# The bias of the score sigmoid, as a constant of the instruction instead of a tile

## The chip, the cores and the metric

The kernel runs on one core of a Trainium2 chip. The metric is the device time of one execution in microseconds; lower is better. The kernel before takes 389.12 us (median of three runs, 388.84 to 390.28).

## The reference

Two layers stand one behind the other. The first is attention with a sigmoid in the place of the softmax, on 8 batches of 12 heads, 448 positions and 64 channels:

```
scores = scale * np.matmul(q, k.transpose(0, 1, 3, 2)) - np.log(S)
attn = 1.0 / (1.0 + np.exp(-scores))
attn_out = np.matmul(attn, v)
```

The subtracted logarithm of S = 448 is the same number, about 6.1048, for every score. The second layer is dense, on 3584 tokens of 768 channels (all heads of a position side by side):

```
h = x @ w_in
g = h * (1.0 / (1.0 + np.exp(-beta * h)))
out = g @ w_out
```

`w_in` is 768 x 2048, `w_out` is 2048 x 768, and `beta` has one number per column of `h`. Inputs and output are float32.

## The kernel before

**Loading.** The DMAs that GpSimd issues load q and k (the tile `raw`, lines 105 to 117), v, `w_in` and `w_out`, and turn them into fp16 on the way. Each group of four heads (a "quad", 24 in all, three to a batch) is then transposed by VectorE in blocks of 32 (`qT`, `kT`, lines 179 to 194). SyncE issues only the load of beta and the stores.

**Scores and sigmoid.** `score` (L201) multiplies 32 rows of `kT` with 32 rows of `qT`, for four heads at once in four strips of the array, into a PSUM tile `sco` of two banks (two heads, up to 448 positions each). `weigh` (L212) is one ScalarE activation on that tile: sigmoid(0.125 x score + bias), written as fp16 to `attnT`. It reads the bias from the tile `nlogs`, one float32 per partition, all equal. There are 171 of these activations: 165 on 896 elements per partition and 6 on 448. `visit` and `half_visit` issue the scores of two `sco` tiles and then their two activations, which so come in pairs. In the first stage there are three `sco` tiles, later two, so that the scores of the next visit can begin only when the pair before has read its tiles.

**The weighted sum and the dense layer.** `attend` (L267) multiplies `attnT` with v, and VectorE copies the result to `xT` (L276). `dense1` (L285) is `x @ w_in` into a PSUM bank; ScalarE makes `sg`, the sigmoid with the scale taken from the tile `beta_sb` and a constant bias of zero (L293); VectorE multiplies the two into `gt` (L296), which sets the bank free. `dense2` (L315) is `g @ w_out` for the first three and the last of the 28 row blocks; the others go through seven products of sums in place of eight (`strassen`, L397 with the sums of L386, L416, L419 and L421).

**The order.** It is written out by hand: within `tc.manual_schedule()` each engine executes its instructions in the order in which they are issued in the source. The first stage (lines 496 to 560) loads the quads of batch 0 in halves and fills TensorE's waits with multiplications of a tile of zeros (`idle_units`, L509). After it, the visits of the other quads alternate with units of the dense layer, which a list with costs in microseconds (`filler_stream`, `spread`, `rest`) deals out between them; from line 595 on a visit is followed by so many units as its budget allows. The list and its costs are fixed in the source and do not depend on what an instruction takes on the chip.

**Around the change.** GpSimd's first instructions are two loads, the two `memset` of lines 498 (`nlogs`) and 499 (`dummy`), and then the loads of the second and third quad. The activation on `dummy` (L500) lets ScalarE load its table of functions while the first data are on their way. `nlogs` is the first tile of the pool `const`.

Of the kernel before, what the change touches and what calls it, by code (L numbers as in the profile page):

```python
# [8 lines left out]
FP32 = mybir.dt.float32  # L9
# [4 lines left out]
def kernel(  # L14
# [10 lines left out]
    nc = tc.nc  # L25
# [6 lines left out]
    P = 128  # L32
# [16 lines left out]
    NEG_LOG_S = -math.log(float(S))  # L49
# [3 lines left out]
    const = ctx.enter_context(tc.tile_pool(name="const", bufs=1))  # L53
# [35 lines left out]
        return psum["one"].tile([P, cols], FP32, tag=f"one{i}", name=name)  # L89


    nlogs = const.tile([P, 1], FP32, name="nlogs")
    dummy = const.tile([P, 1], FP32, name="dummy")
    beta_in = const.tile([BLK, P], FP32, name="beta_in")
    beta_sb = const.tile([P, BLK], FP32, name="beta_sb")
# [11 lines left out]
    def load_one(g: int, r: int, c0: int = 0, c1: int = NB):  # L107
        b, t = divmod(g, QPB)
        if g not in raws:
            raws[g] = rawp.tile([P, 2, NB, D], FP16, tag="raw", name="raw")  # L110
        nc.gpsimd.dma_start(  # L111
            out=raws[g][:, r, c0:c1].rearrange("p c d -> p (c d)"),
            in_=(q, k)[r][b, HQ * t : HQ * (t + 1)].rearrange("h (p c) d -> (h p) (c d)", c=NB)[
                :, c0 * D : c1 * D
            ],
        )
# [93 lines left out]
    def weigh(sco, n: int):  # L210
        at = attnp.tile([P, 2, S], FP16, tag="attnT", name="attnT")
        nc.scalar.activation(  # L212
            out=at[:, :, 0:n],
            in_=sco[:, :, 0:n],
            func=AF.Sigmoid,
            bias=nlogs[:, 0:1],
            scale=MSCALE,
        )
        return at


    def visit(g: int, jt: int, also=()):
        if jt < JF:
            todo = [(score_tile(), [s]) for s in (2 * g, 2 * g + 1)]
        else:
            todo = [(score_tile(), [2 * h, 2 * h + 1]) for h in (g, *also)]
        for e in range(PAIR):
            for sco, slots in todo:
                for s in slots:
                    for hh in range(2):  # L230
                        score(sco, 0, s, jt, hh, e, 0, S)
        for sco, slots in todo:
            at = weigh(sco, S)
            for s in slots:
                at_tiles[s, jt, 0] = at


    def half_visit(g: int, c0: int, second: int):
        slots = (2 * g, 2 * g + 1)
        scos = [score_tile() for _ in slots]  # L240
        plan = [(s, jt, sco, jt * QH) for jt in (0, 1) for s, sco in zip(slots, scos)]
        widths = [S, S]
        if second:
            plan = [(s, 2, sco, 0) for s, sco in zip(slots, scos)]
            plan += [(s, JF, scos[0], QH) for s in slots]
            widths = [S, QH]
        for i in range(0, len(plan), 2):
            for e in range(PAIR):
                for s, jt, sco, u0 in plan[i : i + 2]:
                    for hh in range(2):  # L250
                        score(sco, u0, s, jt, hh, e, c0, QH)
        ats = {id(sco): weigh(sco, n) for sco, n in zip(scos, widths)}
        for s, jt, sco, u0 in plan:
            at_tiles[s, jt, c0] = ats[id(sco)][:, :, u0 : u0 + QH]
# [240 lines left out]
    with tc.manual_schedule():  # L495
        load_one(0, 0, 0, NH)
        load_one(0, 1)
        nc.gpsimd.memset(nlogs, NEG_LOG_S)  # L498
        nc.gpsimd.memset(dummy, 0.0)  # L499
        nc.scalar.activation(out=dummy, in_=dummy, func=AF.Sigmoid, bias=0.0, scale=1.0)  # L500

# [156 lines left out]
```

## Time and profile before

| | |
|---|---|
| time, median of three runs | 389.12 us |
| the three runs | 390.28, 389.12, 388.84 us |
| span of the profiled execution | 388.2 us |
| the profiled execution's own time | not listed apart from the three runs; the span is 0.9 us below their median |
| TensorE busy | 381.5 us (98%) |
| ScalarE busy | 241.5 us (62%), of which L212 is 160.3 us |
| VectorE busy | 229.7 us (59%) |
| granted TensorE clock | 1.00 over the span |

The span runs from the first to the last instruction on the core. Around it lies what the trace does not hold, the launch and the end of the program. Busy shares are means over stages with different limits, and TensorE's busy time counts a matmul from its start to a modelled end, in which the next has already begun. What another engine's speed is worth is thus read from the places where TensorE stands still, and from what ended each of them.

### The profile page before, as it was taken

To read this page: it belongs to the slowest core of one execution; us is meant where nothing else is said; L and a number is where in the kernel's file an instruction comes from. 1 tells how busy PE (TensorE), PEld (TensorE's weight loads), DVE (VectorE), ACT (ScalarE), POOL (GpSimd) and SP (SyncE) were. 2 spreads that over 40 slices of the span, in tenths; PEclk is the share of its full clock that TensorE was granted. 3 is DMA by queue.
4 is the path that set the end of the run, shared out by engine and by line. 5 is a ranking of instruction groups with operands and counts; after the bars stand their busy time and mean duration, and the time that the engine had idled before them with its cause. 6 is when DMAs were issued, how large, how long until landed. Compare 5 with 4: busy or idle time off the path is not lost.

```text
span 388.2 us, 7376 instructions
## 1 busy us (share of the span) xinstructions
PE 381.5 (98%) x2991; PEld 191.4 (49%) x2991; DVE 229.7 (59%) x437; ACT 241.5 (62%) x329; POOL 67.3 (17%) x117
## 2 busy tenths in 40 slices
PE   8899999999999999999999999999999999999996
PEld 3477754444545444444554445544445444555563
DVE  2356463885766556655765656664676565655762
ACT  4887865687565796497365783568853677625200
POOL 7833343122110410140110410104100000000000
PEclk9999999999999999999999999999999999999999
DMA  7999999629243760446353561629113300030033
GB/s 112 172 191 203 198 204 199 144 55 112 47 91 70 126 80 14 105 79 66 49 115 74 87 71 34 127 60 144 28 21 83 82 2 2 0 83 0 2 81 122
DMA packets 42401, 34.30 MB, mean 88 GB/s; under 512 B 21872, under 2 KB 38784, under 8 KB 42368
## 3 DMA queue, kind: packets, MB, share of 16 engines
q0 software_dynamic: 36976, 22.81, 42.8%
q1 hardware_dynamic: 5392, 11.02, 11.0%
q8 instruction: 23, 0.38, 0.4%
q14 instruction: 10, 0.08, 0.1%
HBM read 45.62 MB, written 11.01 MB: 146 GB/s over the span
## 4 chain that ended last, share of the span: by engine, by line
PE 93%; DMA 3%; ACT 2%; POOL 0%; issue 0%; DVE 0%; POOLq 0%
PE m_ps L285 39%; PE m_ps L397 29%; PE sco L201 11%; PE av_ps L267 10%; PE m_ps L315 4%; ACT attnT L212 2%; DMA raw<-in_k_dram 2%; DMA v<-in_v_dram 1%; POOL raw L111 0%; PE idle_ps L509 0%; ACT sg L293 0%; DVE osb L328 0%; DVE gt L296 0%; POOL nlogs L498 0%; POOL dummy L499 0%
## 5 line engine op out<-in xcount | busy, mean ns | idle before, releaser
L212 ACT ACTIVATE attnT<-sco,nlogs 128x896 f16<-128x896 f32 (+1 forms) x171 | 160.3, 991 | 84.3 <-PE sco L201 83.5
L285 PE MATMUL m_ps<-xT,w_in 128*128 128x448 f16 (+1 forms) x864 | 154.7, 332 | 0.4 <-DVE gt L296 0.3
L296 DVE TENSOR_TENSOR gt<-m_ps,sg 128x448 f16<-128x448 f32 (+1 forms) x144 | 79.8, 572 | 84.4 <-ACT sg L293 84.3
L285 PEld LDWEIGHTS <-w_in 128*128 128x128 f16 x864 | 80.6, 98 | 70.9 <-issue 15.5
L293 ACT ACTIVATE sg<-m_ps,beta_sb 128x448 f32<-128x448 f32 (+1 forms) x144 | 81.8, 595 | 31.3 <-PE m_ps L285 30.1
L397 PEld LDWEIGHTS <-sum 128*128 128x128 f16 x480 | 45.2, 98 | 36.4 <-issue 7.9
L201 PE MATMUL sco<-qT,kT 32*128 32x448 f16 (+3 forms) x864 | 52.6, 340 | 1.3 <-ACT attnT L212 1.1
L397 PE MATMUL m_ps<-w_T,sum 128*128 128x384 f16 x288 | 51.6, 327 | 0.0
L111 POOL DMA_DIRECT2D raw<-in_q_dram x27 | 14.8, 550 | 189.7 <-DVE kT L191 183.1
L416 DVE TENSOR_TENSOR osb<-m_ps,osb 128x384 f32<-128x384 f32 x60 | 33.3, 555 | 18.7 <-PE m_ps L397 16.9
L267 PE MATMUL av_ps<-attnT,v 128*64 128x448 f16 (+3 forms) x432 | 42.2, 340 | 0.7 <-DMA v<-in_v_dram 0.5
L276 DVE CAST xT<-av_ps 128x448 f16<-128x448 f32 (+1 forms) x54 | 28.8, 568 | 22.5 <-PE av_ps L267 22.5
L386 DVE TENSOR_TENSOR sum<-gt 128x1024 f16<-128x1024 f16 x60 | 39.1, 678 | 0.1
L397 PE MATMUL m_ps<-w_T,gt 128*128 128x384 f16 x192 | 34.2, 327 | 0.0
L397 PE MATMUL m_ps<-w_out,sum 128*128 128x384 f16 x192 | 33.7, 326 | 0.0
L267 PEld LDWEIGHTS <-v 128*64 128x64 f16 (+1 forms) x432 | 19.1, 107 | 25.5 <-issue 16.9
L201 PEld LDWEIGHTS <-kT 32*128 32x128 f16 (+1 forms) x864 | 13.5, 96 | 29.6 <-issue 27.5
L397 PEld LDWEIGHTS <-gt 128*128 128x128 f16 x192 | 18.1, 98 | 14.8 <-issue 3.1
L315 PE MATMUL m_ps<-w_out,gt 128*128 128x384 f16 (+2 forms) x128 | 22.5, 327 | 0.0
L132 POOL DMA_DIRECT2D v<-in_v_dram x32 | 19.8, 635 | 8.0 <-DMA w_in<-in_moe_w_in_dram 5.3
L179 DVE STREAM_TRANSPOSE qT<-raw 128x448 f32<-128x448 f32 (+1 forms) x27 | 16.6, 616 | 4.8 <-DMA raw<-in_q_dram 4.8
L315 PEld LDWEIGHTS <-gt 128*128 128x128 f16 x128 | 11.9, 98 | 10.3 <-issue 3.1
(24 smaller groups left out, 96.9 us busy)
## 6 DMA issues: line engine op xcount, KB each, us to landing
out_dram<-osb SPq DMA_DIRECT2D x98, 96.0 KB, 1.9
raw<-in_k_dram POOLq DMA_DIRECT2D x24, 224.0 KB, 4.8
raw<-in_q_dram POOLq DMA_DIRECT2D x21, 224.0 KB, 3.6
v<-in_v_dram POOLq DMA_DIRECT2D x32, 144.0 KB, 6.6
w_in<-in_moe_w_in_dram POOLq DMA_DIRECT2D x8, 384.0 KB, 10.9
w_out<-in_moe_w_out_dram POOLq DMA_DIRECT2D x4, 768.0 KB, 13.4
v<-in_v_dram POOLq DMA_DIRECT2D x16, 48.0 KB, 6.2
out_dram<-osb SPq DMA_DIRECT2D x2, 384.0 KB, 2.3
```

What stands on the lines that cost most here:

```text
L132: nc.gpsimd.dma_start(out=vs[b][i * BLK : (i + 1) * BLK, :, 0:JF].rearrange("p h j d -> p h (j d)"), in_=rows[:, :, JF * i * D : JF * (i + ...
L201: nc.tensor.matmul(sco[base : base + nk, hh, u0 : u0 + n], kT[g][lo : lo + BLK, jt * P : jt * P + nk, e], qT[g][lo : lo + BLK, c0 : c0 + n ...
L212: nc.scalar.activation(out=at[:, :, 0:n], in_=sco[:, :, 0:n], func=AF.Sigmoid, bias=nlogs[:, 0:1], scale=MSCALE,)
L267: nc.tensor.matmul(av[hh * D : (hh + 1) * D, 0:n], vs[b][base : base + nk, 2 * (s % NPAIR) + hh, jt], at[base : base + nk, hh, 0:n], start ...
L276: nc.vector.tensor_copy(out=xTs[b][:, s % NPAIR, c0 : c0 + n], in_=av[:, 0:n])
L285: nc.tensor.matmul(m1[:, 0:n], w_in16[:, hc, dc * P : (dc + 1) * P], xTs[b][:, hc, c0 : c0 + n], start=(hc == 0), stop=(hc == NHC - 1),)
L293: nc.scalar.activation(out=sg[:, 0:n], in_=m1[:, 0:n], func=AF.Sigmoid, bias=0.0, scale=beta_sb[:, dc : dc + 1])
L296: nc.vector.tensor_tensor(out=gt[:, dc, off : off + n], in0=m1[:, 0:n], in1=sg[:, 0:n], op=ALU.mult)
L315: nc.tensor.matmul(m2, gt[:, dc, cols(t)], w_out16[:, dc, lo:hi], start=(dc == 0), stop=(dc == NDC - 1),)
L386: nc.vector.tensor_tensor(out=sums[t, i], in0=x, in1=y, op=op)
L397: nc.tensor.matmul(m2, (x if op is None else sums[t, i])[:, dc], w[:, dc], start=first and dc == 0, stop=(dc == ND - 1), skip_group_check= ...
L416: nc.vector.tensor_tensor(out=out, in0=in0, in1=in1, op=op)
```

## The change

The activation of `weigh` takes its bias from the instruction, as a float constant, in place of the tile. The tile `nlogs` and its `memset` go.

```
-    nlogs = const.tile([P, 1], FP32, name="nlogs")
     dummy = const.tile([P, 1], FP32, name="dummy")
...
             func=AF.Sigmoid,
-            bias=nlogs[:, 0:1],
+            bias=NEG_LOG_S,
             scale=MSCALE,
...
         load_one(0, 1)
-        nc.gpsimd.memset(nlogs, NEG_LOG_S)
         nc.gpsimd.memset(dummy, 0.0)
```

In the built program, 171 activations have a constant operand where they had an access pattern, GpSimd has one instruction less, and the activation on `dummy` waits for GpSimd's count to be 1 where it was 2. Every other instruction, its engine, its place and its waits stay as they were. The tiles move in one respect: the pool places tiles in steps of 32 bytes per partition, so each tile behind `nlogs` (all but the constants ahead of it) starts 32 bytes lower in its partition: `w_in16` at 17184 in place of 17216, `gt` at 66336 in place of 66368. In the kernel before the starts of the large tiles are multiples of 64; in the kernel after each is 32 off such a multiple.

More of the change, by code (lines that the diff above doesn't have):

```diff
@@ L89, in bank @@
         return psum["one"].tile([P, cols], FP32, tag=f"one{i}", name=name)
-    nlogs = const.tile([P, 1], FP32, name="nlogs")
     dummy = const.tile([P, 1], FP32, name="dummy")
@@ L215, in weigh @@
             func=AF.Sigmoid,
-            bias=nlogs[:, 0:1],
+            bias=NEG_LOG_S,
             scale=MSCALE,
@@ L497 @@
         load_one(0, 1)
-        nc.gpsimd.memset(nlogs, NEG_LOG_S)
         nc.gpsimd.memset(dummy, 0.0)
```

## The prediction

> **What bounds the kernel now.** I read the page's head and its chain of waits first, then the stretches of the span, then TensorE's own waits, because the change touches ScalarE and the question is where TensorE stands still for it. The page:
>
> ```profile
> span 388.2 us, 7376 instructions
> PE 381.5 (98%) x2991; PEld 191.4 (49%) x2991; DVE 229.7 (59%) x437; ACT 241.5 (62%) x329; POOL 67.3 (17%) x117
> PE 93%; DMA 3%; ACT 2%; POOL 0%; issue 0%; DVE 0%; POOLq 0%
> ```
>
> The chain that ended last runs 93% on TensorE and 2% on ScalarE: ScalarE matters only at a few places. Which, the stretches show (length, then busy time of each engine with its instructions, granted clock, DMA share, GB/s):
>
> ```profile
> 0.00:18.00 18.00, 15.65 (x157) 6.22 (x159) 5.18 (x15) 11.42 (x14) 14.10 (x28) 1.00 1.08 141
> 18.00:38.00 20.00, 19.96 (x273) 14.39 (x266) 11.24 (x33) 16.64 (x29) 7.93 (x12) 1.00 1.36 193
> 38.00:76.00 38.00, 36.83 (x331) 20.75 (x329) 22.00 (x46) 26.00 (x37) 11.96 (x20) 1.00 1.20 186
> 76.00:343.00 267.00, 267.00 (x2002) 126.46 (x1999) 166.91 (x303) 176.35 (x232) 33.33 (x58) 1.00 0.41 68
> 343.00:388.20 45.20, 42.11 (x244) 23.59 (x241) 24.32 (x42) 11.09 (x18) 0.00 (x0) 1.00 0.19 57
> ```
>
> From 76 to 343 us TensorE is busy for 267.00 of 267.00 us. Whatever ScalarE gains there, TensorE has nothing to give back. The last stretch has no score activation in it. The same view for the instructions of `attnT` alone (TensorE's, then ScalarE's) has in that stretch
>
> ```profile
> 76.00:343.00 267.00, 29.76 (x292) 119.84 (x126) 1.00 0.41 68
> ```
>
> so 126 of the 171 activations run under a full TensorE. What is left is 2.35 us of TensorE's idle time before 18 us and 1.17 us between 38 and 76 us. TensorE's waits name what ended it:
>
> ```profile
> PE sco L201 <- ACT attnT L212: 1.1, 4, 0.3
> PE av_ps L267 <- DMA v<-in_v_dram: 0.5, 1, 0.5
> PE m_ps L285 <- DVE gt L296: 0.3, 1, 0.3
> ```
>
> Four waits of scores for ScalarE make 1.1 us in total, and one wait of the dense layer for VectorE 0.3 us. The chain in order of time (start, length) gives the places of the four:
>
> ```profile
> 16.65 1.02 ACT attnT L212
> 17.71 0.57 PE sco L201 x14
> ...
> 56.37 1.89 ACT attnT L212 x2
> 58.31 0.57 PE sco L201 x6
> ...
> 61.50 1.89 ACT attnT L212 x2
> 63.43 0.59 PE sco L201 x12
> ...
> 68.21 1.89 ACT attnT L212 x2
> 70.15 0.57 PE sco L201 x6
> ```
>
> At 17.71 the scores wait for one activation, at 58.31, 63.43 and 70.15 for the end of a pair. The fifth wait is behind ScalarE too, as the timeline shows (start, length, engine, line, idle time before and what ended it):
>
> ```profile
> 47.64 1.90 ACT L212 ACTIVATE attnT<-sco,nlogs 128x896 f16<-128x896 f32 x2 [1.56 <-PE sco L201]
> 49.43 1.46 ACT L293 ACTIVATE sg<-m_ps,beta_sb 128x224 f32<-128x224 f32 x4
> 49.91 1.40 DVE L296 TENSOR_TENSOR gt<-m_ps,sg 128x224 f16<-128x224 f32 x4 [2.22 <-ACT sg L293]
> 50.36 1.31 PE L285 MATMUL m_ps<-xT,w_in 128*128 128x224 f16 x12 [0.35 <-DVE gt L296]
> ```
>
> TensorE needs a bank that VectorE frees (50.36, after 0.35 us idle); VectorE waits for the sigmoid `sg`; and that stands in ScalarE's queue behind a pair of score activations.
>
> **What one activation loses.** Forms of instructions, with their busy us and the mean ns of one ahead of the last bar:
>
> ```profile
> L212 ACT ACTIVATE attnT<-sco,nlogs 128x896 f16<-128x896 f32 x165 | 157.2, 1004 | 84.3 <-PE sco L201 83.5
> L419 ACT COPY osb<-m_ps 128x384 f32<-128x384 f32 x12 | 5.7, 478 | 15.5 <-PE m_ps L397 15.3
> L212 ACT ACTIVATE attnT<-sco,nlogs 128x448 f16<-128x448 f32 x6 | 3.8, 627 | 0.0
> L500 ACT ACTIVATE dummy<-dummy 128x1 f32<-128x1 f32 x1 | 0.2, 203 | 0.6 <-POOL dummy L499 0.6
> ```
>
> The two sizes of L212 give (1004 - 627) / 448 = 0.84 ns per element and a fixed part of 1004 - 896 x 0.8415 = 250 ns. No row has a score sigmoid with a constant bias, so its fixed part is bounded. The copy of L419 reads PSUM and has no tile beside its input: 478 - 384 x 0.8415 = 155 ns, 95 ns less. The activation on `dummy` is a sigmoid whose bias and scale are both constants: 203 - 1 = 202 ns, 48 ns less. The upper end is 95 ns, the lower zero (a constant could also cost something; no row gives a reason, and I leave that to the slower cases). I take 95 ns: the copy streams a PSUM tile through the engine as L212 does, while the 203 ns are for one element in SBUF. The Trainium skill, "ScalarE: Activation LUTs", section "What ACT_TABLE_LOAD costs", puts an activation with constant scale and bias at 186 ns plus 0.833 ns per element, and each operand read from a tile at some 93 ns more; by that the same sum would come out at 0.88 us instead of 0.90. The trace agrees to 2 ns if the copy is the right neighbour, and not if `dummy` is.
>
> **Does a pair lose it twice?** A pair takes 1.90 us and not twice 1.004: the second begins about 0.11 us before the end of the first. If that overlap were the reading of the bias tile, taking the read away would shorten only the last of a run. One row speaks on this:
>
> ```profile
> 152.84 1.90 ACT L212 ACTIVATE attnT<-sco,nlogs 128x896 f16<-128x896 f32 x2 [1.27 <-PE sco L201]
> 154.64 0.48 ACT L419 COPY osb<-m_ps 128x384 f32<-128x384 f32 x1
> ```
>
> The pair ends at 154.74, and the copy, which reads no such tile, starts at 154.64, 0.10 us earlier, as early as an activation does. The overlap belongs to the end of the instruction in front, not to the next one's operand. So I let each activation of a pair lose 95 ns, the pair 0.19 us.
>
> **The sum.** (1) At 17.71: one activation, 0.095 us. (2) At 58.31, 63.43 and 70.15: 3 x 0.19 = 0.57 us. (3) At 50.36: the `sg` behind the pair starts 0.19 us earlier, and so do VectorE and TensorE. Each cut is smaller than the idle time that it meets (1.1 us over the four waits, 0.35 us at 50.36), so all of it counts and the waits remain, shorter. (4) The start:
>
> ```profile
> 2.40 0.13 POOL L498 MEMSET nlogs<- 128x1 f32 x1
> 2.44 0.13 POOL L499 MEMSET dummy<- 128x1 f32 x1
> 2.48 0.55 POOL L111 DMA_DIRECT2D raw<-in_q_dram  x1
> 3.00 0.56 POOL L111 DMA_DIRECT2D raw<-in_k_dram  x1
> ```
>
> ```profile
> 3.00 6.24 DMA raw<-in_k_dram
> 9.52 5.49 DMA v<-in_v_dram
> 15.43 0.54 PE idle_ps L509 x2
> ```
>
> The removed memset stands in GpSimd's queue ahead of every load from the second quad on, and the chain goes through the k load issued at 3.00, the v load of 9.52 that waits for it, and the sum that needs v. From one memset's start to the next instruction's is 0.04 us; that is the gain, between nothing and the memset's whole 0.13 us. Before 15.43 the chain runs over loads alone, so shorter activations there only wait longer for v; if the v load came sooner than they end, they would be the next in line. `dummy`'s activation, 0.04 us earlier, is waited for by nothing but ScalarE's own first pair, which waits for scores. Nothing on SyncE's queue moves.
>
> 0.095 + 0.57 + 0.19 + 0.04 = 0.90 us. By the lower price of 48 ns it would be 9 x 0.048 + 0.04 = 0.47 us. ScalarE's busy time falls by 171 x 0.095 = 16 us, of which nearly all turns into idle time: its cover is the full TensorE from 76 to 343 us, and if that cover were gone the 16 us would be the most that could come out. The sum is against the profiled span: 388.2 to 387.3 us. The span lies 0.9 us below the median of the runs; with the same distance kept the time is 389.12 - 0.90 = 388.2 us. The three runs differ by 1.4 us, so 0.5% (1.95 us) is about what a measurement of this kernel can tell from no change.
>
> **Rivals.** *The overlap is the read after all.* The starts in a run keep their spacing and only its last end comes earlier: 4 x 0.095 + 0.04 = 0.42 us, nothing at 50.36, 388.7 us; with no shorter activation at all 389.1 us, the case in which the change does not do what it says. For it: the overlap (0.10 to 0.11 us) is about as large as the price. The same section of the Trainium skill states an overlap of some 93 ns for activations in a row, the figure that it gives for the operand too; taken as one and the same thing, that makes this rival. Against it: the copy at 154.64.
>
> *The addresses.* Every large tile moves from a multiple of 64 bytes to 32 beyond one. If a matmul's reads of SBUF cost more there, the place is wherever TensorE is full, above all 76 to 343 us, and each ns is paid: 2991 matmuls x 1 ns = 3.0 us. From 0.3 ns per matmul on it eats the gain of 0.90 us, from 0.95 ns on the kernel is slower by 0.5%; at 1.2 ns the time is 391.8 us. In this trace no tile read by a matmul starts off such a multiple, so its price has no row; the only thing near is that the memsets of `nlogs` (a multiple of 64) and of `dummy` (32 beyond one) both take 0.13 us in the rows above. The Trainium skill, "SBUF — State Buffer", section "Specifications (TRN2)", gives cachelines of 16 bytes, which a step of 32 leaves as they were; no run here shows it yet.
>
> *More than the sum.* If the activations lose so much that all five waits vanish, the idle times before them go, 1.1 + 0.3 = 1.4 us, with the start 387.7 us. Faster by over 0.5% needs about 0.5 us more, and only the loads of the first 16 us could give that, by landing sooner; the k load took 6.24 us and the v load 5.49 us, and a tenth less of both is 1.2 us. The same transfers can as well land later.
>
> **How the numbers follow.** The forecast of 388.2 us (its own range 387.5 to 389.0) has 0.50; the overlap or no effect 0.22 (388.7 to 389.1); the addresses 0.09 and a start with later loads 0.05 (over 390); more than the sum 0.14 (387.7 down to 386.7). Faster by over 0.5% (below 387.17) takes most of that last case and a tail of the forecast, 0.12; slower (above 391.07) the addresses and half of the later loads, 0.12; within 0.5% is left with 0.76. The range from 387.0 to 390.4 leaves the addresses, half of the later loads and half of the large gain outside.
>
> **What would show it.** In the changed profile: L212 on 128x896 near 0.91 us, pairs near 1.71 us, ScalarE busy near 225 us; the waits of scores for ScalarE down from 1.1 to about 0.45 us and the wait behind `gt` from 0.35 to 0.16; TensorE still full from about 75 us on, and the same time for 2002 matmuls there as before (267 us). If that stretch is longer, the addresses are at work and the prediction is wrong; if pairs keep their spacing of 0.9 us, the overlap rival holds; if the matmuls of zeros behind the first sum with v begin more than 0.3 us away from 15.43 us, the loads decide.

## The result and the profile after

The changed kernel takes 388.69 us (median of 22 runs) against 389.78 us before (22 runs, the three shown above among them). One of the 22 runs of the changed kernel took 960.06 us, for a reason that the record does not give; the ratio leaves it out, and the median of the other 21 is 388.62 us. The ratio is 0.9974, 95% interval 0.9967 to 0.9980: 1.01 us faster (0.78 to 1.29). (The ratio is not the quotient of the medians, which lie 1.09 us apart.) That is a gain clear of the noise, and it is under 0.5%.

The page after, its head, the activations of L211 (L212 before) by form with busy us and mean ns, and TensorE's waits:

```profile
span 387.3 us, 7375 instructions
PE 381.3 (98%) x2991; PEld 191.5 (49%) x2991; DVE 231.5 (60%) x437; ACT 228.9 (59%) x329; POOL 67.4 (17%) x116
```

```profile
L211 ACT ACTIVATE attnT<-sco 128x896 f16<-128x896 f32 x165 | 142.6, 915 | 89.8 <-PE sco L200 89.2
L418 ACT COPY osb<-m_ps 128x384 f32<-128x384 f32 x12 | 5.8, 480 | 16.7 <-DMA out_dram<-osb 8.6 <-PE m_ps L396 8.1
L211 ACT ACTIVATE attnT<-sco 128x448 f16<-128x448 f32 x6 | 3.2, 538 | 0.0
```

```profile
PE av_ps L266 <- DMA v<-in_v_dram: 0.6, 1, 0.6
...
PE sco L200 <- ACT attnT L211: 0.2, 1, 0.2
PE m_ps L284 <- DVE gt L295: 0.2, 1, 0.2
```

An activation takes 915 ns on 896 elements and 538 on 448, 89 ns less than before in both sizes. The waits of scores for ScalarE fall from 1.1 us to one of 0.2 us that the view still lists; it leaves out the three behind it, which have become 0.09 to 0.10 us long, and all four together are 0.48 us, where the prediction said about 0.45. The wait behind `gt` falls from 0.35 to 0.17 us. Where the time came from is best seen in the chain after, in order of time, and in the timeline at the fifth wait:

```profile
16.91 0.93 ACT attnT L211
17.88 0.57 PE sco L200 x13
...
50.16 1.31 PE m_ps L284 x12
...
56.17 1.71 ACT attnT L211 x2
57.93 0.57 PE sco L200 x6
...
61.11 1.72 ACT attnT L211 x2
62.87 0.59 PE sco L200 x12
...
67.65 1.71 ACT attnT L211 x2
69.40 0.57 PE sco L200 x6
```

```profile
47.62 1.73 ACT L211 ACTIVATE attnT<-sco 128x896 f16<-128x896 f32 x2 [1.91 <-PE sco L200]
49.23 1.47 ACT L292 ACTIVATE sg<-m_ps,beta_sb 128x224 f32<-128x224 f32 x4
49.71 1.40 DVE L295 TENSOR_TENSOR gt<-m_ps,sg 128x224 f16<-128x224 f32 x4 [2.04 <-ACT sg L292]
50.16 1.31 PE L284 MATMUL m_ps<-xT,w_in 128*128 128x224 f16 x12 [0.17 <-DVE gt L295]
```

The same matmuls stood at 17.71, 50.36, 58.31, 63.43 and 70.15 us. The lead over the kernel before is thus -0.17, 0.20, 0.38, 0.56 and 0.75 us: each pair between 50 and 70 us adds 0.18 to 0.19 us. At the end of the span it is 0.9 us.

### The profile page after: what moved, and what is told of

Its sections match the earlier page's. It is cut to its first block, busy times and chain, and to the rows that moved or that the text cites. A ratio compares the mean times of both kernels' runs of the same rounds, so it can differ in the third digit from the quotient of the medians.

```text
span 387.3 us, 7375 instructions
## 1 busy us (share of the span) xinstructions
PE 381.3 (98%) x2991; PEld 191.5 (49%) x2991; DVE 231.5 (60%) x437; ACT 228.9 (59%) x329; POOL 67.4 (17%) x116
## 4 chain that ended last, share of the span: by engine, by line
PE 93%; DMA 3%; ACT 2%; issue 1%; POOL 0%; DVE 0%; ACTq 0%; POOLq 0%
PE m_ps L284 38%; PE m_ps L396 29%; PE sco L200 11%; PE av_ps L266 10%; PE m_ps L314 5%; ACT attnT L211 2%; DMA raw<-in_k_dram 2%; DMA v<-in_v_dram 1%; POOL raw L110 0%; PE idle_ps L507 0%; ACT sg L292 0%; DVE osb L327 0%; DVE gt L295 0%; POOL dummy L497 0%; ACTq L292 0%
## 5 line engine op out<-in xcount | busy, mean ns | idle before, releaser
L211 ACT ACTIVATE attnT<-sco 128x896 f16<-128x896 f32 (+1 forms) x171 | 145.2, 902 | 89.8 <-PE sco L200 89.2
L295 DVE TENSOR_TENSOR gt<-m_ps,sg 128x448 f16<-128x448 f32 (+1 forms) x144 | 81.7, 572 | 81.2 <-ACT sg L292 77.2
L292 ACT ACTIVATE sg<-m_ps,beta_sb 128x448 f32<-128x448 f32 (+1 forms) x144 | 84.4, 596 | 36.3 <-PE m_ps L284 31.0
L200 PEld LDWEIGHTS <-kT 32*128 32x128 f16 (+1 forms) x864 | 13.4, 96 | 28.7 <-issue 26.9
```

Of the source, the lines that this page charges most:

```text
L200: nc.tensor.matmul(sco[base : base + nk, hh, u0 : u0 + n], kT[g][lo : lo + BLK, jt * P : jt * P + nk, e], qT[g][lo : lo + BLK, c0 : c0 + n ...
L211: nc.scalar.activation(out=at[:, :, 0:n], in_=sco[:, :, 0:n], func=AF.Sigmoid, bias=NEG_LOG_S, scale=MSCALE,)
L292: nc.scalar.activation(out=sg[:, 0:n], in_=m1[:, 0:n], func=AF.Sigmoid, bias=0.0, scale=beta_sb[:, dc : dc + 1])
L295: nc.vector.tensor_tensor(out=gt[:, dc, off : off + n], in0=m1[:, 0:n], in1=sg[:, 0:n], op=ALU.mult)
```

## The experiments

Ratios are to the kernel before on the same chip, with the 95% interval. A lead is read by setting TensorE's matmuls of the two traces beside each other, one by one: the start before less the start of the same matmul here.

**The constant with the tile kept.**

```
-            bias=nlogs[:, 0:1],
+            bias=NEG_LOG_S,
             scale=MSCALE,
```

The tile `nlogs` and its `memset` stay.

> Constant bias, but the tile of the bias, its memset and with them all addresses and GpSimd's order stay as before. Theory (the operand's 0.09 us per activation at the places where TensorE waits for ScalarE): the whole gain of the change but 0.04 us, some 0.8 to 1.0 us, a ratio near 0.9975. Rival (the addresses or the missing memset bring the gain): no gain, ratio 1.000.

388.44 us, ratio 0.9972 (0.9962 to 0.9982); activations at 915 ns. The gain is there with all addresses and GpSimd's order as before. It is the operand's.

**The addresses alone.**

```
-    nlogs = const.tile([P, 1], FP32, name="nlogs")
+    nlogs = const.tile([P, 9], FP32, name="nlogs")
...
-        nc.gpsimd.memset(nlogs, NEG_LOG_S)
+        nc.gpsimd.memset(nlogs[:, 0:1], NEG_LOG_S)
```

> The bias stays a tile, now 36 bytes wide, so that every tile behind it starts 32 bytes off a multiple of 64, as in the changed kernel. Theory: no change, ratio within 0.0007 of 1.000, 2002 matmuls from 76 to 343 us still in 267 us. Rival (addresses matter): up to 1 us faster if they bring the gain; or slower by some ns for each of 2991 matmuls, over 3 us, if they had eaten a part of a larger gain.

389.77 us, ratio 1.0003 (0.9993 to 1.0012). The stretch from 76 to 343 us, and the activations by form:

```profile
76.00:343.00 267.00, 267.00 (x2000) 126.52 (x2001) 167.14 (x303) 176.47 (x232) 33.35 (x58) 1.00 0.41 68
```

```profile
L212 ACT ACTIVATE attnT<-sco,nlogs 128x896 f16<-128x896 f32 x165 | 157.3, 1005 | 83.9 <-PE sco L201 83.2
```

TensorE does 2000 matmuls there (2002 before), and one activation takes 1005 ns (1004). The first sum with v comes 0.27 us earlier than before in this profile, and matmul for matmul the two traces stay 0.27 to 0.28 us apart up to the end; the stretch moved by as much, from 75.72 to 342.72 us, holds 2002 matmuls again. Tiles that start 32 bytes off a multiple of 64 cost the matmuls here nothing that these runs can tell, and bring nothing.

**The constant in the first 46 activations only**, and **in the last 125 only.**

```
+    weighed = [0]
+
     def weigh(sco, n: int):
+        weighed[0] += 1
...
-            bias=nlogs[:, 0:1],
+            bias=NEG_LOG_S if weighed[0] <= 46 else nlogs[:, 0:1],
```

In the second of the two kernels the constant and the tile change places in the last line. What was expected of the first, then of the second:

> Constant bias only in the first 46 activations, those before 76 us; the 125 behind keep the tile. Theory: nearly all of the gain, 0.8 to 0.95 us, though ScalarE's busy time falls by only 4 us. Rival (the gain follows ScalarE's total work): 46 of 171 parts of 1.0 us, 0.27 us.

> The reverse: the first 46 activations keep the tile, the 125 from 76 us on have the constant. Theory: about 0.1 us, from the one place near 236.7 us where the sum of a product comes late; ScalarE's busy time falls by 11 us. Rival (the gain follows ScalarE's total work): 125 of 171 parts of 1.0 us, 0.73 us.

The first 46: 388.58 us, ratio 0.9974 (0.9965 to 0.9983), with ScalarE at 238.0 us busy. The last 125: 389.61 us, ratio 1.0002 (0.9993 to 1.0010), with ScalarE at 232.8 us. Two and a half times the saved work on ScalarE (8.7 against 3.5 us), and none of the gain that a measurement can tell. The lead of the second kernel has one step, 0.10 us at the matmul that stood at 236.70 us before. The forms of the two, first the kernel with the constant in the first 46:

```profile
L215 ACT ACTIVATE attnT<-sco,nlogs 128x896 f16<-128x896 f32 x125 | 119.0, 1004 | 65.8 <-PE sco L201 65.7
L215 ACT ACTIVATE attnT<-sco 128x896 f16<-128x896 f32 x40 | 35.0, 917 | 20.1 <-PE sco L201 19.5
```

```profile
L215 ACT ACTIVATE attnT<-sco 128x896 f16<-128x896 f32 x125 | 107.7, 914 | 68.9 <-PE sco L201 68.8
L215 ACT ACTIVATE attnT<-sco,nlogs 128x896 f16<-128x896 f32 x40 | 38.4, 1007 | 18.5 <-PE sco L201 17.8
```

**One operand more instead of one less.**

```
-    nlogs = const.tile([P, 1], FP32, name="nlogs")
+    nlogs = const.tile([P, 2], FP32, name="nlogs")
...
-            scale=MSCALE,
+            scale=nlogs[:, 1:2],
...
+        nc.gpsimd.memset(nlogs[:, 1:2], MSCALE)
```

> The scale of the score activation is read from a tile too (a second column beside the bias, one more memset). Theory (each operand read from a tile lengthens an activation by 0.09 us, in a row as well as alone): 896 elements take 1.09 us, a pair 2.08 us; the five waits, the hidden one at 26.4 us and the one at 236.7 us grow by what they lost in the change or a little more, 1.0 to 1.6 us slower, ratio 1.0026 to 1.004. Rival (a second scalar is fetched beside the first): 0.04 us for the memset, ratio 1.000.

392.44 us, ratio 1.0060 (1.0046 to 1.0073): 2.3 us slower by the ratio (1.8 to 2.8), 2.75 us by the medians of 5 and 15 runs, and in any case more than the 1.0 to 1.6 expected. The price of the operand is as expected, the form takes 92 ns more than before:

```profile
L212 ACT ACTIVATE attnT<-sco,nlogs 128x896 f16<-128x896 f32 x165 | 172.2, 1096 | 79.1 <-PE sco L201 78.6
```

The seven known places cost 0.17 to 0.18 us each, 1.3 us in all; at 17.71 that is twice what the change gained, since here ScalarE runs seven activations without a break from 12.1 us on. What was not expected is a place at 43.2 us, worth some 0.08 us, and six new places behind 76 us, each worth 0.17 to 0.18 us: at 110, 115, 196, 244, 257 and 305 us of the kernel before, together about 1.1 us. At the first, TensorE's timeline before, and then here, shows a group of eight score matmuls; the line of ScalarE ahead of them is the second activation of the pair that they follow before:

```profile
109.17 1.00 ACT L212 ACTIVATE attnT<-sco,nlogs 128x896 f16<-128x896 f32 x1
```

```profile
108.83 1.46 PE L397 MATMUL m_ps<-w_T,sum 128*128 128x384 f16 x8
110.22 0.57 PE L201 MATMUL sco<-qT,kT 32*128 32x448 f16 x8
110.73 1.47 PE L397 MATMUL m_ps<-w_T,sum 128*128 128x384 f16 x8
```

```profile
109.68 1.79 PE L397 MATMUL m_ps<-w_T,sum 128*128 128x384 f16 x10
111.40 0.76 PE L201 MATMUL sco<-qT,kT 32*128 32x448 f16 x8
112.09 1.48 PE L397 MATMUL m_ps<-w_T,sum 128*128 128x384 f16 x8
```

The group takes 0.76 us in place of 0.57, with no idle time shown: a stall of 0.19 us inside a busy stretch. Before, the pair ends at 110.17 and the scores start 0.05 us later, as soon after a pair as at the wait of 58.31 (the pair of 56.37 ends at 58.26): the place had just enough room for a pair of 1.90 us and not for one of 2.09. So in this kernel more work on ScalarE costs more than less work brings.

**A shorter sigmoid in the dense layer.** The scale beta is replaced by 1.0, so this kernel leaves beta out.

```
-            out=sg[:, 0:n], in_=m1[:, 0:n], func=AF.Sigmoid, bias=0.0, scale=beta_sb[:, dc : dc + 1]
+            out=sg[:, 0:n], in_=m1[:, 0:n], func=AF.Sigmoid, bias=0.0, scale=1.0
```

> Bias tile as before; the sigmoid of the dense layer takes the constant scale 1.0 in place of beta, so beta is left out of the computation. Theory: 144 activations lose 0.09 us each, 13 us of ScalarE's busy time, nearly as much as in the change; but only the waits behind them count, at 50.36 and 236.7 us, 0.1 to 0.2 us in all, ratio 0.9995. Rival (the gain follows ScalarE's total work): 0.8 us, ratio 0.998.

389.40 us, ratio 0.9992 (0.9983 to 1.0000), 0.3 us with an interval from nothing to 0.7, so the ratio alone does not exclude the rival by much. The trace does: the form loses 92 ns (635 to 543), and TensorE's lead grows at two places behind the start, 0.09 us at 50.36 and 0.09 us at 236.70.

```profile
L293 ACT ACTIVATE sg<-m_ps 128x448 f32<-128x448 f32 x112 | 60.7, 543 | 32.8 <-PE m_ps L285 31.8
```

ScalarE's busy time is 233.1 us, 8.4 less than before and not 13: added one by one the activations are 13.4 us shorter, but those in a row overlap, by 20.8 us in all before and by 15.8 us here, so that more of each is counted.

**The waits that are left.** The units of the second layer are cut in two, in the changed kernel and, as a control, in the kernel before.

```
-    N2 = 4
+    N2 = 8
...
-                fill_units(3)
-                spent += 3 * M2_US / N2
+                fill_units(6)
+                spent += 6 * M2_US / N2
```

Expected of the constant with finer units, of the same again, of the tile with finer units, and of the changed kernel again:

> The changed kernel, with the units of the plain second layer cut in two (two matmuls in place of four), so that the visits between 56 and 76 us are followed by about 10 matmuls each in place of 12 and 8 in turn. Theory: the three waits that are left at the pairs of 57.9, 62.9 and 69.4 us, about 0.28 us each with the part that the modelled ends hide, go; 0.5 to 0.9 us faster than the changed kernel, ratio to before 0.9950 to 0.9965. Rival (the finer dealing moves banks and later visits, and opens waits elsewhere): no faster than the changed kernel, ratio 0.997 or above.

> Constant bias and finer units again, beside the run with the tile on one chip. Theory: ratio to before near 0.994, span near 385.6 us.

> The kernel before, bias from the tile, with the finer units alone. Theory (TensorE waits wherever the pair of 1.90 us outlasts the matmuls dealt between two visits): with 10 matmuls between all visits the three waits of 0.46 us become some six of about 0.13 us; 0.4 to 0.8 us faster than before, ratio near 0.9985, and the constant bias is then worth 1.2 to 1.8 us on top of it, more than its 1.0 us with the coarse units. Rival (the finer units remove these waits with either bias): 1.3 us faster or more, ratio 0.9965 or less, and the constant worth 0.9 us or less.

> The changed kernel itself, beside the others on one chip. Theory: ratio 0.9975 to before, span 387.0 to 387.5; the start of the first sum with v moves by some tenths of a us from profile to profile, since only a load ends it.

The first two rows of the table ran on one chip (before 389.69 us there), the last two on another (before 389.61 us).

| | us | ratio |
|---|---|---|
| changed kernel again | 388.49 | 0.9963 (0.9951 to 0.9976) |
| constant, finer units | 387.38 | 0.9938 (0.9926 to 0.9951) |
| the same again | 387.61 | 0.9946 (0.9933 to 0.9958) |
| tile, finer units | 388.90 | 0.9982 (0.9973 to 0.9991) |

Constant and finer units together are the fastest kernel of this study, 1.1 us ahead of the changed one beside it; 0.5 to 0.9 was expected. The changed kernel again came out faster than expected too, with a span of 386.7 us for 387.0 to 387.5 and a ratio whose interval just holds 0.9975; in its profile the first sum with v came early. In TensorE's timeline of the changed kernel, as first profiled, 8 matmuls of the second layer and the scores behind them, which wait:

```profile
56.05 1.48 PE L314 MATMUL m_ps<-w_out,gt 128*128 128x384 f16 x8
57.45 1.04 PE L200 MATMUL sco<-qT,kT 32*128 32x448 f16 x8
```

With the finer units 10 matmuls stand between the visits, and the scores nearly run on:

```profile
55.28 1.80 PE L314 MATMUL m_ps<-w_out,gt 128*128 128x384 f16 x10
57.01 0.72 PE L200 MATMUL sco<-qT,kT 32*128 32x448 f16 x8
57.66 1.80 PE L314 MATMUL m_ps<-w_out,gt 128*128 128x384 f16 x10
59.40 0.58 PE L200 MATMUL sco<-qT,kT 32*128 32x448 f16 x8
```

With the tile, the timeline of that control shows the same visits:

```profile
56.12 1.80 PE L315 MATMUL m_ps<-w_out,gt 128*128 128x384 f16 x10
57.86 0.90 PE L201 MATMUL sco<-qT,kT 32*128 32x448 f16 x8
58.69 1.80 PE L315 MATMUL m_ps<-w_out,gt 128*128 128x384 f16 x10
60.42 0.72 PE L201 MATMUL sco<-qT,kT 32*128 32x448 f16 x8
```

Its scores take 0.90 and 0.72 us in place of 0.72 and 0.58; eight that wait for nothing take 0.57. So a part of the waits stays in both, 0.33 and 0.15 us a group with the tile, where some six waits of 0.13 us were expected. The finer units alone brought 0.7 us (0.4 to 0.8 expected). On the same chip the constant is worth 388.90 - 387.61 = 1.3 us with the finer units (1.2 to 1.8 expected), at the low end. By the times alone that can't be told from its 1.0 us with the coarse units; by the traces it is 0.15 us more, since the steps of the lead behind the first sum with v add up to 1.25 us, and to 1.1 with the coarse units. The lead grows by 0.69 us between 50 and 72 us, in five steps where the coarse units have three; a pair of 1.73 us nearly fits between two such visits and one of 1.90 does not.

## Why the prediction was right, point by point

**The price of the operand**, 95 ns from the copy of L419, measured 89. The lower price from `dummy`, 48 ns, is out: the fixed part that is left is 915 - 896 x 0.8415 = 161 ns, near the copy's 155 and not `dummy`'s 202. Why `dummy` takes longer is not shown; it differs in its one element and in reading SBUF. The change gives 89 less, the second operand 92 more, the constant scale of `sg` 92 less (635 to 543). This is the figure of the Trainium skill, "ScalarE: Activation LUTs", section "What ACT_TABLE_LOAD costs", some 93 ns for each operand read from a tile. The fixed part of 186 ns, which the prediction quotes from the same section of the Trainium skill, is 25 ns more than the 161 measured here.

**The pair loses it twice.** Right; ScalarE's timeline after:

```profile
152.10 1.73 ACT L211 ACTIVATE attnT<-sco 128x896 f16<-128x896 f32 x2 [1.45 <-PE sco L200]
153.71 0.49 ACT L418 COPY osb<-m_ps 128x384 f32<-128x384 f32 x1
```

A pair takes 1.73 us (1.90 before), and what follows still starts 0.12 us before its end (153.71 against 153.83), now that no activation of the pair reads a tile. The overlap was not the read, and the rival that said so is out.

**The five places.** Right in place and size: 0.09 us at 17.71 (the activation takes 0.93 us in the chain and not 1.02), 0.18 to 0.20 us at 50.36 and 0.18 at each of the three pairs, against 0.095 and 0.19.

**TensorE has nothing to give back from 76 to 343 us.** Wrong by 0.10 us, and the same step missed 0.17 us at 26.4 us. The argument took a busy share of 267.00 of 267.00 us for work without a stall. A matmul is counted up to a modelled end, while the next may long have begun, as the form of the scores before shows:

```profile
L201 PE MATMUL sco<-qT,kT 32*128 32x448 f16 x504 | 36.9, 360 | 0.6 <-ACT attnT L212 0.6
```

504 matmuls of 360 ns make 36.9 us of busy time, 73 ns each. Four at once in the four strips would make 90; the rest is that the next four begin before the counted ends. So a short stall leaves no gap: those found here were of 0.10 to 0.19 us. At 26.4 us, a pair on ScalarE and TensorE's timeline before, and TensorE's after:

```profile
24.42 1.90 ACT L212 ACTIVATE attnT<-sco,nlogs 128x896 f16<-128x896 f32 x2
26.19 0.88 PE L201 MATMUL sco<-qT,kT 32*128 32x224 f16 x16
```

```profile
26.36 0.70 PE L200 MATMUL sco<-qT,kT 32*128 32x224 f16 x16
```

The same 16 matmuls take 0.18 us less: they had waited for the pair, which ended at 26.32, 0.05 us before the matmul whose lead jumps (26.38). At 236.70 the weights of a product waited 0.32 us for a sum, and after the change no more:

```profile
236.70 1.25 PEld L397 LDWEIGHTS <-sum 128*128 128x128 f16 x9 [0.32 <-DVE sum L386]
```

```profile
235.77 1.32 PEld L396 LDWEIGHTS <-sum 128*128 128x128 f16 x9
```

The sum comes from `gt`, that from `sg`, and `sg` stood behind a pair on ScalarE, as at 50.36:

```profile
232.96 1.90 ACT L212 ACTIVATE attnT<-sco,nlogs 128x896 f16<-128x896 f32 x2
234.76 0.63 ACT L293 ACTIVATE sg<-m_ps,beta_sb 128x448 f32<-128x448 f32 x1
```

The kernel with the constant in the last part has this step and no other, the one with the constant in the first part has all the others and not this one, and the one with the constant scale has it beside that at 50.36.

**The start.** The issue moved as said; whether it brings 0.04 us can't be seen. The chain after:

```profile
2.96 6.33 DMA raw<-in_k_dram
9.57 5.70 DMA v<-in_v_dram
15.69 0.54 PE idle_ps L507 x2
```

The k load is issued at 2.96 in place of 3.00, lands 0.05 us later, and the matmuls of zeros behind the sum with v stand at 15.69 in place of 15.43, which is within the 0.3 us that the prediction allowed the loads. In the twelve profiles of this study these matmuls begin between 14.65 and 15.62 us in the timeline (15.36 before; 15.62 and 14.93 in two profiles of the changed kernel). The start moves by up to a us between profiles, and 0.04 us drowns in it.

**The sum.** From 17 us on, where the loads no longer decide, the measured steps are 0.09 + 0.17 + 0.20 + 3 x 0.18 + 0.10 = 1.1 us, against 0.86 predicted; 0.26 us of later loads take the profiled span back to the 0.9 that was forecast, by chance. Over 22 runs of each the gain is 1.01 us (0.78 to 1.29), which holds the 1.1 of the steps and the forecast of 0.90 alike. The forecast of 388.2 us stood on the three runs' median of 389.12; with more runs the kernel before stands at 389.78. That is 0.66 us higher; less the 0.19 us by which the gain of the medians was larger than forecast (389.78 - 388.69 = 1.09), it leaves the 0.5 us between 388.2 and 388.69. ScalarE's busy time fell by 12.6 us and not by 16: added one by one the activations lost 15.0 us, at 89 ns and not 95, and their overlaps fell from 20.8 to 18.4 us, above all between sigmoids of the dense layer.

**The rivals.** The addresses are out by the run that moved them alone. A gain beyond the sum through the loads was not seen.

## What to carry to other kernels

A saving on an engine off the critical path is worth what the waits behind that engine give, place by place: here 9 of 171 activations were forecast to bring nearly the whole gain, and the first 46 did. Read such places from the chain and the waits, and check a busy stretch of TensorE for groups of equal matmuls that take longer than their like, since the modelled ends hid stalls of up to 0.19 us here. What is left of a wait may be a matter of how filling work is dealt out: with 10 matmuls after each visit in place of 12 and 8, the shorter activations were worth 1.3 us, and both together 2.0 to 2.3 us.

## What was not expected of the hardware

The cost is lopsided: 89 ns less per activation brought 1.0 us, 92 ns more took 2.3 us, above all because six places behind 76 us had room for a pair of 1.90 us with next to nothing to spare. And the first loads land so unevenly (the matmuls behind the sum that needs v begin over a stretch of 1.0 us in twelve profiles) that no step at the start of some hundredths of a us can be told.
